# Linear attention and a gelu MLP on one core: batch 2's q mapped and transposed in two halves, and some steps of iteration 1 moved

## The chip, the cores and the metric

The kernel runs on one core of a Trainium2 chip. The metric is the device time of one execution in microseconds (us); the median of five runs is compared. TensorE is called PE in the profile, VectorE DVE, ScalarE ACT, GpSimd POOL and SyncE SP; SP's queue carries the loads and the DMA transposes here, ACT's queue the stores.

## The reference

Eight batches of eight heads, 576 positions, head width 64, go through linear attention; the result is the input of a two-layer MLP with 4608 rows, width 512 and inner width 2048:

```
phi(x) = where(x > 0, x, exp(x) - 1) + 1          # per element
kv  = phi(k)^T v ;  z = sum over positions of phi(k)
x   = (phi(q) kv) / (phi(q) z + 1e-6)             # per batch and head
h   = x @ w_in ;  g = gelu_tanh(h) ;  out = g @ w_out
```

## The kernel before, in words

phi(x) is made as min(max(x + 1, 1), exp(x)). So a map of q or k is three steps: `exp_of` on ACT, `linear_of` (add 1, maximum with 1) on DVE, `least_of` (the minimum of the two) on DVE. Tiles are [128 positions, chunks, heads, 64]: q has four chunks of 128 positions (the last 64 positions of each batch are handled later, two batches together), k has nine pieces.

For one batch the stages are: kv (`kv_paired`, 72 small matmuls into a pair of PSUM banks of its own, then casts into `kvbd` or `kv`); q transposed by DMA, chunk by chunk (`least_q`, from SP, into `qt`); n, the product of qt and kv (`nab`, one chunk at a time, L266), whose last column is the denominator; the division (`divide`, a reciprocal and a multiplication on DVE, L283 and L284) into `xs`; xs transposed by DMA into `xt` (`transposed_x`, L686); then the MLP on xt.

The MLP of one batch is an iteration of `iteration(j)`. It has 16 h tiles m0 to m15 (`h_mm`, L390, four matmuls of 128x512 each into one bank), each followed by a gelu on ACT (L405), and the output product. From iteration 1 on, the output product is made by seven half-size products of sums and differences (Winograd's form of Strassen's method): `sum_w_out` makes the sums of the weights once (L744), `Products.sums`, `third_sum` and `last_sum` those of g (L755, on DVE), and `Products.step(n)` one product of 16 matmuls (L782) and what follows it: a copy on ACT (L810, L823) or an addition on DVE (L851). Product 1's bank `p` is copied, and product 2 later accumulates into the same bank, so that bank is held from product 1 to the copy after product 2.

The order on every engine is written out by hand. `iteration(j)` makes a list of steps, and each step is a slot. Other work is put behind a slot with `at(j, slot, fn, ...)`, and `run(j, slot)` emits it, in the order in which it was registered; the plans of batches 2 and 3 are registered before those of the iteration itself. Iteration 1's slots are:

```
0-7: h m0-m7   8: product 1   9: product 7   10-17: h m8-m15   18-22: products 2, 6, 5, 4, 3
```

So h tile m11 is slot 13 and m13 is slot 15. In iteration 2 the h tiles alternate, m0, m8, m1, m9, and so on. While iteration 1 runs, the kernel prepares batch 2 (`plan_third`: its maps, kv at slot 12, n of chunks 0 to 3 at slots 15, 17, 18 and 18) and begins batch 3 and k of batch 4 (`plan_fourth`). An ACT table must be loaded when ACT changes between exp and gelu (L220 and L418).

h, the products and other one-bank tiles share six PSUM banks; a pair of banks of its own serves kv and most n tiles, one at a time. `load_*` calls put loads on SP's queue, seven buffers in turn; `least_q` also issues its four DMA transposes there (L663). The exp tile of k (`k_e`) has one buffer, so the exp of the next batch's k waits for the minimum that reads the one before.

Of the kernel before, what the change touches and what calls it, by code (L numbers as in the profile page):

```python
# [16 lines left out]
def kernel(  # L17
# [16 lines left out]
    nc = tc.nc  # L34
# [175 lines left out]
        n, hn = ld[name, b].shape[2] // D, ld[name, b].shape[1]  # L210
        phi[name, b] = pphi.tile([P, n, hn, D], BF16, name=name + "_p")

    def exp_of(name, b, hs=None):
        x = ld[name, b]
        hs = hs or slice(0, x.shape[1])
        if (name, b) not in exps:
            e = name + ("_e" if name != "qr" or b % 2 else "_f")
            exps[name, b] = pe.tile([P, x.shape[2] // D, x.shape[1], D], BF16, name=e)
        o, i = maps_view(name, b, x, exps[name, b], hs)
        nc.scalar.activation(o, i, AF.Exp)  # L220

    def linear_of(name, b, hs=None):
# [4 lines left out]
        o, i = maps_view(name, b, x, phi[name, b], hs)  # L227
        nc.vector.tensor_scalar(o, i, 1.0, 1.0, op0=ALU.add, op1=ALU.max)  # L228

    def least_of(name, b, hs=None):  # L230
        p, e = phi[name, b], exps[name, b]
        if hs:
            p, e = p[:, :, hs, :], e[:, :, hs, :]
        nc.vector.tensor_tensor(p, p, e, op=ALU.min)  # L234


# [276 lines left out]
    def at(j, slot, fn, *args):  # L513


        fill.setdefault((j, slot), []).append((fn, args))
# [74 lines left out]
    def plan_third():  # L591
        def n(c):
            transposed_x(2, c, (nab_in_banks if c == 3 else nab)(qts[2], 2, c))

        at(1, 1, sum_w_out, slice(0, 2))
        at(1, 2, linear_of, "k", 2)
        at(1, 3, linear_of, "q", 2)
        at(1, 4, cast_v, 2)
        at(1, 7, exp_of, "k", 2)
        at(1, 7, exp_of, "q", 2)  # L600
        at(1, 7, gelu_table)
        at(1, 9, least_of, "k", 2)
        at(1, 9, least_q, 2)
        at(1, 9, load_all_pairs, "k", k, 4)
        at(1, 12, kv_in_pair, 2)
        for c, slot in enumerate((15, 17, 18, 18)):
            at(1, slot, n, c)

    def plan_fourth():

        at(1, 12, linear_of, "k", 3)
        at(1, 17, exp_of, "k", 3)
        at(1, 18, exp_of, "q", 3)
        at(1, 18, exp_of, "k", 4)
        at(1, 18, gelu_table)
        at(1, 21, linear_of, "q", 3)
        at(1, 22, least_of, "k", 3)
        at(2, 0, cast_v, 3)
        at(2, 0, least_q, 3)
        at(2, 4, kv_in_pair, 3)  # L620
        at(2, 5, linear_of, "k", 4)
        at(2, 5, least_of, "k", 4)
        at(2, 5, cast_v, 4)
        at(2, 8, linear_of, "q", 4)
        at(2, 15, exp_of, "q", 4)
        at(2, 16, exp_of, "k", 5)
        at(2, 19, least_q, 4)
        at(2, 22, linear_of, "k", 5)
        at(3, 0, least_of, "k", 5)
# [26 lines left out]
        at(j, 15, exp_of, "qr", m)  # L656
        at(j, 18, least)

    def least_q(b):
        least_of("q", b)  # L660
        qts[b] = pt.tile([P, C, NP, P], BF16, name="qt")
        for c in range(C):
            nc.sync.dma_start_transpose(  # L663
                out=qts[b][:, c],
                in_=phi["q", b][:, c].rearrange("p h d -> p (h d)"),
            )
# [81 lines left out]
    class Products:  # L748
# [42 lines left out]
        def step(self, name):  # L791

            j = self.j
            (a11, a12), (a21, a22) = self.a
            (b11, b21), (t3, b22) = [[w_out_sb[:, d, h] for h in ff] for d in range(2)]
            t1, t2, t4 = (w_sum[:, i] for i in range(3))
            lo, hi = slice(0, N2), slice(N2, d_model)
            self.done = getattr(self, "done", ()) + (name,)

            def new():  # L800
                if name == 5 and j == B:
                    return [bank("o_ps", [P, N2]) for _ in range(2)]
                return bank("o_ps", [P, 2, N2])

            if name == 1:
                self.p = new()
                self.product(self.p, a11, b11, True)
                self.o1 = pout.tile([P, 2, d_model], FP32, name="o_sb")
                self.o2 = pout.tile([P, 2, d_model], FP32, name="o_sb")
                nc.scalar.copy(self.o1[:, :, hi], self.p)  # L810
            elif name == 5:
                self.z = new()
                self.product(self.z, self.s[0], t1, True)
            elif name == 6:
                v = new()
                self.product(v, self.s[1], t2, True)
                self.plus(self.o1[:, :, hi], v, self.o1[:, :, hi])
            elif name == 7:
                self.w = new()
                self.product(self.w, self.s3, t3, True)  # L820
            elif name == 2:
                self.product(self.p, a12, b21, False)
                nc.scalar.copy(self.o1[:, :, lo], self.p)  # L823
                if j == B:
                    self.store(0, self.o1, lo)
            elif name == 4:
                self.product(self.w, a22, t4, False)
                self.plus(self.o2[:, :, lo], self.w, self.o1[:, :, hi])
                self.store(1, self.o2, lo if j == B else slice(0, d_model))
            elif name == 3 and j < B:  # L830
                self.product(self.z, a11, b22, False)
                self.plus(self.o1[:, :, hi], self.z, self.o1[:, :, hi])
                at(j + 1, 0, self.store, 0, self.o1)
            elif name == 3:
                for t in range(2):
                    self.product(self.z, a11, b22, False, (t,))
                    self.plus(self.o1[:, t, hi], self.z[t], self.o1[:, t, hi])
                    self.store_rest(t, self.o1[:, t], hi)
            both = {6, 7} <= set(self.done)
            if name in (6, 7) and both:  # L840
                self.plus(self.o2[:, :, hi], self.w, self.o1[:, :, hi])
            if name in (5, 6, 7) and both and 5 in self.done:
                if j < B:
                    self.plus(self.o2[:, :, hi], self.z, self.o2[:, :, hi])
                else:
                    for t in range(2):
                        self.plus(self.o2[:, t, hi], self.z[t], self.o2[:, t, hi])
                    self.store(1, self.o2, hi)
# [20 lines left out]
    def iteration(j):  # L869
        xt = xts[j]  # L870
        if j < B:
            g = pg.tile([P, 2, MM, MAIN // 2], FP16, name="g")
        else:
            g = pg.tile([P, MM, 2, MAIN // 2], FP16, name="g").rearrange("p m a n -> p a m n")
        hs = [("h", m) for m in range(MM)]
        us = [range(m, m + 4) for m in range(0, MM, 4)]
        products = Products(j, g) if j else None
        early, late = slice(0, MM // 4), slice(MM // 4, MM // 2)
        if j == 0:
            us[2:3] = range(8, 10), range(10, 12)  # L880
            steps = hs + [("o", t, u) for u in us for t in range(C)]
        elif j == 1:
            steps = hs[:8] + [("product", n) for n in (1, 7)]
            steps += hs[8:] + [("product", n) for n in (2, 6, 5, 4, 3)]
            at(1, 7, products.third_sum, early, False)
            at(1, 7, products.third_sum, late, False)
            at(1, 7, sum_w_out, slice(2, 4))
            at(1, 13, products.sums, early)
            at(1, 17, products.sums, late)
            at(1, 19, products.last_sum)  # L890
        else:
            steps = [hs[i + n] for i in range(MM // 2) for n in (0, MM // 2)]
            steps += [("product", n) for n in (1, 5, 6, 7, 2, 4, 3)]
            for slot, ms in ((7, early), (15, late)):
                at(j, slot, products.sums, ms)
                at(j, slot, products.third_sum, ms)
            at(j, 16, products.last_sum)
        o_pss = {}
        for slot, step in enumerate(steps):
            if step[0] == "h":  # L900
                m = step[1]
                h_ps = h_begun.get(j, {}).get(m)
                if h_ps is None:
                    h_ps = bank("h_ps", [P, MAIN])
                    h_mm(h_ps, xt, m)
                gelu(j, g, m, h_ps)
            elif step[0] == "product":
                products.step(step[1])
            else:
                t, u = step[1:]  # L910
                if u.start == 0:
                    o_pss[t] = bank("o_ps", [P, d_model])
                o_mm(o_pss[t], g, t, u, half=(j, slot - 0.5))
                if u.stop == MM:
                    finish(j, t, o_pss[t])
            run(j, slot)
# [54 lines left out]
```

## Time and profile before

| | before |
|---|---|
| median of five runs | 272.74 us (272.39 to 272.83) |
| profiled execution | 272.4 us, of which span 270.6 us |
| PE busy | 264.2 us (98%) |
| PE weight load busy | 170.4 us (63%) |
| DVE busy | 164.9 us (61%) |
| ACT busy | 165.5 us (61%) |
| granted TensorE clock | 1.00 |
| iteration 1, first h to last product | 47.8 to 76.5 us |

Times in a timeline are counted from the start of the span. A row gives the start, the length, the engine, the line of the kernel, the operation and its tiles; equal neighbours are merged, with their number behind an x, and in brackets stands the idle time of the engine before the row with what ended it. Lengths of neighbouring instructions overlap: an h matmul is recorded with 0.38 us, but the next one starts 0.2155 us later. What an engine loses is therefore read from distances between starts.

### The profile page before, as it was taken

The numbers are of one execution on the slowest core, as the hardware profiler recorded it, in microseconds if no ns is written. First come the engines' busy times: TensorE is split into PE (matmuls) and PEld (weight loads), VectorE is DVE, ScalarE is ACT, GpSimd is POOL, SyncE is SP. The second block draws the span as 40 slices with busy tenths as digits, with TensorE's granted clock in tenths as the row PEclk, the third lists the DMA queues.
The fourth block names the chain that finished last, engine by engine and source line by source line (L and its number), as shares of the span: only waits on it lengthen the run. The fifth ranks groups of instructions, "written<-read, shape, count | busy, mean of one in ns | idle before, by whom it ended". The sixth has DMA issues, their size and how long they took to land.

```text
span 270.6 us, 5936 instructions
## 1 busy us (share of the span) xinstructions
PE 264.2 (98%) x2533; PEld 170.4 (63%) x2533; DVE 164.9 (61%) x263; ACT 165.5 (61%) x224; POOL 15.0 (6%) x21
## 2 busy tenths in 40 slices
PE   8999999999999999999999999999999999999994
PEld 3584456464854686558745874587458745874584
DVE  2860186988998966788738874683267316622262
ACT  4768877798839583669275926581665265028700
POOL 3056401000000000000000000000000000000000
PEclk9999999999999999999999999999999999999999
DMA  6999999993899998996698465217451312121004
GB/s 234 402 406 396 410 407 400 399 365 64 237 310 288 296 254 193 295 327 77 167 361 252 102 157 138 61 39 152 103 41 40 130 65 61 19 111 47 0 0 157
DMA packets 59786, 53.87 MB, mean 199 GB/s; under 512 B 35696, under 2 KB 45936, under 8 KB 59760
## 3 DMA queue, kind: packets, MB, share of 16 engines
q1 hardware_dynamic: 56880, 44.57, 57.1%
q10 hardware_dynamic: 2880, 8.91, 9.2%
q8 instruction: 20, 0.33, 0.5%
q14 instruction: 6, 0.05, 0.0%
HBM read 36.70 MB, written 9.44 MB: 170 GB/s over the span
## 4 chain that ended last, share of the span: by engine, by line
PE 90%; DMA 4%; ACT 1%; DVE 1%; SPq 1%; issue 0%; ACTq 0%
PE h_ps L390 44%; PE o_ps L782 36%; PE o_ps L726 5%; DMA v_x<-in_v_dram 3%; PE n_ps L328 1%; DMA qt<-q_p 1%; PE n_ps L250 1%; PE n_ps L266 1%; ACT k_e L220 1%; PE kv_ps L250 1%; PE t_ps L383 1%; SPq L94 1%; DVE k_p L234 1%; ACT L418 0%; SPq L99 0%
## 5 line engine op out<-in xcount | busy, mean ns | idle before, releaser
L390 PE MATMUL h_ps<-xt,w_in_sb 128*128 128x512 bf16 (+1 forms) x628 | 128.8, 361 | 0.6 <-ACT g L405 0.5
L405 ACT ACTIVATE g<-h_ps 128x512 f16<-128x512 f32 x144 | 86.2, 618 | 58.1 <-PE h_ps L390 56.2
L390 PEld LDWEIGHTS <-w_in_sb 128*128 128x128 bf16 x628 | 58.1, 98 | 63.1 <-issue 1.1
L782 PEld LDWEIGHTS <-g 128*128 128x128 f16 x624 | 60.9, 98 | 9.0 <-ACT g L405 0.2
L782 PE MATMUL o_ps<-w_out_sb,g 128*128 128x256 f16 x496 | 58.2, 273 | 0.0
L851 DVE TENSOR_TENSOR o_sb<-o_ps,o_sb 128x512 f32<-128x512 f32 (+1 forms) x42 | 27.9, 666 | 29.6 <-PE o_ps L782 28.7
L755 DVE TENSOR_TENSOR s<-g 128x1024 f16<-128x1024 f16 x18 | 12.5, 692 | 39.0 <-ACT g L405 39.0
L782 PE MATMUL o_ps<-w_sum,s 128*128 128x256 f16 x256 | 29.3, 273 | 0.0
L782 PEld LDWEIGHTS <-s 128*128 128x128 f16 x272 | 26.6, 98 | 3.0
L284 DVE TENSOR_TENSOR xs<-n_ps,r 128x384 bf16<-128x384 f32 (+2 forms) x44 | 25.6, 582 | 1.5
L220 ACT ACTIVATE k_e<-k_x 128x2304 bf16<-128x2304 f32 (+1 forms) x9 | 17.2, 1912 | 6.0 <-DVE k_p L234 5.2
L823 ACT COPY o_sb<-o_ps 128x512 f32<-128x512 f32 x8 | 4.7, 584 | 22.3 <-PE o_ps L782 22.3
L228 DVE TENSOR_SCALAR q_p<-q_x 128x2048 bf16<-128x2048 f32 (+1 forms) x9 | 9.9, 1102 | 13.4 <-DMA q_x<-in_q_dram 13.4
L220 ACT ACTIVATE q_e<-q_x 128x2048 bf16<-128x2048 f32 (+1 forms) x9 | 15.5, 1720 | 3.0 <-DMA q_x<-in_q_dram 3.0
L782 PE MATMUL o_ps<-w_sum,g 128*128 128x256 f16 x128 | 15.3, 272 | 0.0
L726 PE MATMUL o_ps<-w_out_sb,g 128*128 128x512 f16 x64 | 15.1, 379 | 0.0
L228 DVE TENSOR_SCALAR k_p<-k_x 128x2304 bf16<-128x2304 f32 (+1 forms) x9 | 11.0, 1220 | 4.2 <-DMA k_x<-in_k_dram 4.1
L418 ACT ACT_TABLE_LOAD x9 | 11.5, 1283 | 0.2
L234 DVE TENSOR_TENSOR k_p<-k_p,k_e 128x2304 bf16<-128x2304 bf16 (+1 forms) x9 | 11.0, 1221 | 0.8 <-ACT k_e L220 0.4
L755 DVE TENSOR_TENSOR s<-s,g 128x1024 f16<-128x1024 f16 x16 | 11.1, 692 | 0.5
L239 DVE CAST vp<-v_x 128x2304 bf16<-128x2304 f32 (+1 forms) x9 | 11.0, 1225 | 0.5 <-DMA v_x<-in_v_dram 0.4
L427 PE MATMUL w_ps<-warm 128*128 128x512 bf16 x32 | 10.0, 469 | 1.2 <-DVE warm L182 1.2
(62 smaller groups left out, 150.7 us busy)
## 6 DMA issues: line engine op xcount, KB each, us to landing
out_dram<-o_sb ACTq DMA_DIRECT2D x16, 512.0 KB, 4.8
k_x<-in_k_dram SPq DMA_DIRECT2D x7, 1152.0 KB, 7.3
v_x<-in_v_dram SPq DMA_DIRECT2D x7, 1152.0 KB, 12.2
q_x<-in_q_dram SPq DMA_DIRECT2D x6, 1024.0 KB, 11.7
w_st<-in_moe_w_in_dram SPq DMA_DIRECT2D x3, 1024.0 KB, 13.2
q_x<-in_q_dram SPq DMA_DIRECT2D x4, 512.0 KB, 8.8
w_st<-in_moe_w_out_dram SPq DMA_DIRECT2D x2, 1024.0 KB, 12.5
w_st<-in_moe_w_out_dram SPq DMA_DIRECT2D x4, 512.0 KB, 11.3
```

The costliest lines, as they stand in the source:

```text
L220: nc.scalar.activation(o, i, AF.Exp)
L228: nc.vector.tensor_scalar(o, i, 1.0, 1.0, op0=ALU.add, op1=ALU.max)
L234: nc.vector.tensor_tensor(p, p, e, op=ALU.min)
L239: fn(out=vp_paired(b)[:, :, us, 0:D].rearrange("p j u d -> p u j d"), in_=ld["v", b][:, us].rearrange("p u (j d) -> p u j d", d=D),)
L284: nc.vector.tensor_tensor(x_v, n_v[heads + (slice(0, D),)], r[heads + (None,)].to_broadcast(shape + [D]), op=ALU.mult,)
L390: nc.tensor.matmul(h_ps[:, ts], lhsT=w_in_sb[:, c, P * m : P * (m + 1)], rhs=xt[:, c, ts], start=(c == 0), stop=(c == KM - 1), skip_group_ ...
L405: nc.scalar.activation(g_v, h_v, AF.Gelu_apprx_tanh)
L418: nc.scalar.preload_act_table_set("gelu_apprx_tanh_and_others")
L726: nc.tensor.matmul(o_ps, lhsT=g[:, t // 2, m, P * (t % 2) : P * (t % 2 + 1)], rhs=w_out_sb[:, :, m, :], start=(m == 0), stop=(m == MM - 1),)
L755: nc.vector.tensor_tensor(out, i0, i1, op=op)
L782: nc.tensor.matmul(ps[t] if type(ps) is list else ps[:, t, :], lhsT=lhs[:, m, P * t : P * (t + 1)], rhs=rhs[:, m, :], start=(first and m = ...
L851: nc.vector.tensor_tensor(out, i0, i1, op=ALU.add)
```

## The change

In iteration 1, batch 2's q is mapped in two halves of two chunks each: the exp of chunks 0 and 1 comes before the exp of k, that of chunks 2 and 3 behind it; the minimum of the first half is taken at slot 8, with two DMA transposes behind it, that of the second half at slot 9 with the other two. The last of the four weight sums moves from slot 7 to slot 8. kv of batch 2 moves from slot 12 to 13 (behind h m11). The linear part of batch 3's k is taken in two halves of head pairs, at slots 9 and 13, instead of whole at slot 12, and its minimum at slot 20 instead of 22. The ACT copy of product 1 moves from slot 8 to slot 13, and the first sums of g from slot 13 to 14.

```diff
-    def exp_of(name, b, hs=None):
+    def exp_of(name, b, hs=None, cs=None):
...
         o, i = maps_view(name, b, x, exps[name, b], hs)
+        if cs:
+            o, i = o[..., cs, :], i[..., cs, :]
         nc.scalar.activation(o, i, AF.Exp)
...
-    def least_of(name, b, hs=None):
+    def least_of(name, b, hs=None, cs=None):
...
+        if cs:
+            p, e = p[:, cs], e[:, cs]
         nc.vector.tensor_tensor(p, p, e, op=ALU.min)
...
         at(1, 4, cast_v, 2)
+        at(1, 7, exp_of, "q", 2, None, slice(0, 2))
         at(1, 7, exp_of, "k", 2)
-        at(1, 7, exp_of, "q", 2)
+        at(1, 7, exp_of, "q", 2, None, slice(2, C))
         at(1, 7, gelu_table)
+        at(1, 8, least_q, 2, slice(0, 2))
         at(1, 9, least_of, "k", 2)
-        at(1, 9, least_q, 2)
+        at(1, 9, least_q, 2, slice(2, C))
         at(1, 9, load_all_pairs, "k", k, 4)
-        at(1, 12, kv_in_pair, 2)
+        at(1, 13, kv_in_pair, 2)
...
-        at(1, 12, linear_of, "k", 3)
+        for slot, hs in zip((9, 13), halves):
+            at(1, slot, linear_of, "k", 3, hs)
...
+        at(1, 20, least_of, "k", 3)
         at(1, 21, linear_of, "q", 3)
-        at(1, 22, least_of, "k", 3)
...
-    def least_q(b):
-        least_of("q", b)
-        qts[b] = pt.tile([P, C, NP, P], BF16, name="qt")
-        for c in range(C):
+    def least_q(b, cs=slice(0, C)):
+        least_of("q", b, cs=cs)
+        if b not in qts:
+            qts[b] = pt.tile([P, C, NP, P], BF16, name="qt")
+        for c in range(cs.start, cs.stop):
...
-                nc.scalar.copy(self.o1[:, :, hi], self.p)
+                if j == 1:
+                    at(1, 13, nc.scalar.copy, self.o1[:, :, hi], self.p)
+                else:
+                    nc.scalar.copy(self.o1[:, :, hi], self.p)
...
-            at(1, 7, sum_w_out, slice(2, 4))
-            at(1, 13, products.sums, early)
+            at(1, 7, sum_w_out, slice(2, 3))
+            at(1, 8, sum_w_out, slice(3, 4))
+            at(1, 14, products.sums, early)
```

## The prediction, made before the changed kernel was run

> **What bounds the kernel now.** I read the page first. Its engine line and the heaviest group say that TensorE (PE) is busy nearly always, with h and output products:
>
> ```profile
> PE 264.2 (98%) x2533; PEld 170.4 (63%) x2533; DVE 164.9 (61%) x263; ACT 165.5 (61%) x224; POOL 15.0 (6%) x21
> ```
>
> So an edit can give time only where PE waits. The chain of waits in order of time shows two such places after the first batches, both in or just behind iteration 1 (columns: start, length, what):
>
> ```profile
> 60.90 0.71 PE kv_ps L250 x72
> 61.60 0.30 PE h_ps L390
> 61.91 3.06 DMA qt<-q_p
> ...
> 65.02 0.41 PE n_ps L266 x4
> ...
> 77.32 1.36 DVE k_p L234
> 78.68 0.02 issue
> 78.70 2.13 ACT k_e L220
> ```
>
> From 105.22 on the same chain holds nothing but PE until the last store. How much PE loses I take from its timeline around these places, by start-to-start distances (an h matmul takes 0.2155, twelve between 58.14 and 60.83):
>
> ```profile
> 60.83 0.78 PE L250 MATMUL kv_ps<-vp,k_p 64*64 64x65 bf16 x72
> 61.54 1.04 PE L390 MATMUL h_ps<-xt,w_in_sb 128*128 128x512 bf16 x4
> 63.03 1.89 PE L390 MATMUL h_ps<-xt,w_in_sb 128*128 128x512 bf16 x8 [0.46 <-ACT g L405]
> 65.02 0.41 PE L266 MATMUL n_ps<-kvbd,qt 128*128 128x130 bf16 x4
> ```
>
> h11 starts at 61.54, so h12 could at 62.41; it starts at 63.03: **0.62** lost, waiting for gelu 8 to free a bank. h12 and h13 end their issue at 64.76, the first n starts at 65.02: **0.26** lost, for the first transposed chunk of qt, which lands at 64.97. In iteration 2 h10 starts at 81.64 and h3 could at 82.51; the chain has it at 82.79: **0.28** lost, behind gelu 0 (82.14 to 82.75), exp k4 (78.70) and least k3 (77.32). Sum 1.16 us: the ceiling of any gain here. The timelines of ACT, DVE and SP show what stands in front:
>
> ```profile
> 56.66 2.13 ACT L220 ACTIVATE k_e<-k_x 128x2304 bf16<-128x2304 f32 x1
> 58.69 1.90 ACT L220 ACTIVATE q_e<-q_x 128x2048 bf16<-128x2048 f32 x1
> 60.60 1.28 ACT L418 ACT_TABLE_LOAD   x1
> 61.90 0.59 ACT L810 COPY o_sb<-o_ps 128x512 f32<-128x512 f32 x1
> 62.38 3.17 ACT L405 ACTIVATE g<-h_ps 128x512 f16<-128x512 f32 x6
> ```
>
> ```profile
> 60.62 1.23 DVE L234 TENSOR_TENSOR q_p<-q_p,q_e 128x2048 bf16<-128x2048 bf16 x1 [0.44 <-ACT q_e L220]
> ...
> 64.48 0.69 DVE L755 TENSOR_TENSOR s<-g 128x1024 f16<-128x1024 f16 x1 [0.47 <-ACT g L405]
> ```
>
> ```profile
> 61.91 5.89 SPq L663 DMA_TRANSPOSE qt<-q_p  x4
> 67.91 0.52 SPq L94 DMA_DIRECT2D k_x<-in_k_dram  x1
> ```
>
> The copy sits ahead of gelu 8; the four transposes wait for the whole q minimum; the sums of slot 13 wait for gelu 11.
>
> **Part by part.** *ACT, slot 7.* The order becomes exp q2 (two chunks), exp k2, exp q2 (the other two), table, gelu 8. Halves of 1024 occur in the first batch: 1.058 us each against 1.909 whole; with the 0.10 by which neighbouring ACT instructions overlap, the split costs 0.96 + 0.96 - 1.81, about 0.1. Starts: q2a 56.66, k2 57.61, q2b 59.64 (ends 60.70), table 60.72, gelu 8 at 62.01 without the copy in front (before 62.38), its end 62.61, so the bank is free for h12 at 62.66. The nearest rows could make the split cost nothing (60.60 for the table) or 0.2 (two whole lengths): h12 between 62.55 and 62.75.
>
> [...]
>
> *The copy of product 1 (0.59, 0.48 start to start)* goes behind gelu 11 (slot 13). It is hidden there: it ends near 64.5, gelu 13 and 14 then wait for their matmuls anyway (ACT idles 0.77 before 66.32). Its reader, product 2's accumulation, starts after 66.5. If that cover were gone it would cost 0.48.
>
> *DVE, slots 7 to 9.* sum_w_out is only divided between slots: no cost. q2a's minimum (0.69, first batch) runs at 57.75, in the idle time before least k2; then the last weight sum until 59.59. least k2 waits for exp k2, now 0.95 later: 59.77 to 61.13. The rest of q2's minimum 61.04 to 61.73, first half of linear k3 (0.75) to 62.40; k3 landed at 58.91.
>
> *PE, kv.* It moves from behind h10 to behind h11. h11 starts at 60.73 (h10 at 59.87), kv at 61.69, 0.56 after its keys are ready, and ends issue at 62.40: it fills most of the hole that stood there. h12 starts at 62.66, **0.37** earlier. Evacuation of kv (two casts, 0.86) 62.50 to 63.36, second half of linear k3 until 64.14.
>
> *SP.* Two transposes can be issued at 58.4 instead of 61.91. All loads ahead of them have been issued, but v3 is still moving (landed 61.58). The pair issued in traffic at 81.14 landed at 87.16, 1.67 behind the q4 load (85.49); the one at 61.91 needed 3.06. So chunk 0 lands between 61.5 (58.4 + 3.06) and 64.4 (58.4 + 6.0, the longest of all qt rows); I take 63.0, v3's end plus 1.5. n0 wants it at 62.66 + 1.72 + 0.03 = 64.41 and kvbd at 63.4: no wait is left, and n0 is **0.60** earlier. The second pair issues at 61.75 and lands by about 66.2; n2 uses it after 68. The k4 load behind them then issues near 64.3 instead of 67.91, and xt's transposes queue behind a load that is finished sooner: no cost, no gain, since xt lands at 75.93 against a need at 76.5.
>
> *What is late next: n1.* It uses the bank pair of n0 and so waits for n0's division on DVE, and that stands behind the two sums of slot 13, now slot 14, which need gelu 11 (start 63.46, end 64.07; before 64.44). Sums start at 64.11 against 64.48; from there to the end of the division the rows take 2.39 (64.48 to 66.87): 66.50, n1 at 66.55. PE could at 66.42. Before it was 67.02. So only **0.47** of the 0.60 survives iteration 1 (0.3 if DVE's extra halves come 0.15 later, 0.60 if it keeps up).
>
> *End of iteration 1.* least k3 moves ahead of two output additions. Before, exp k4 idled 5.20 for it; now it runs after the addition of product 5 (74.02 before, 73.55 now), at 74.2 to 75.5. exp k4 then ends at 77.7, the table at 79.0, gelu 0 at 79.6, against h3's need at 82.0: the **0.28** goes, with 2.4 to spare. The additions of products 4 and 3 come 0.5 later relative to PE; product 4's bank is free at 76.1 and product 3's at 77.9. Banks are handed out again in the order in which they were freed, so these two go to the fifth and sixth h of iteration 2, which start at 79.5 and 81.2: 3.4 and 3.3 of margin. The store that waits for product 4's addition is issued from ACT's queue at about 76.2, ahead of gelu 0, and holds nothing up. DVE's work up to the divisions of iteration 2 keeps its sum.
>
> Sum: 0.47 + 0.28 = 0.75. The profiled execution took 272.4 (span 270.6), the median of the runs 272.74, 0.34 more; I carry the difference over: 272.74 - 0.75 = **272.0**.
>
> **Rivals.** *Little arrives.* PE is at 98%, and 0.47 of the gain passes through three engines' handshakes. If n0 or n1 waits as late as before (qt chunk 0 near 65, or DVE's sums not sooner), only the 0.28 stays: 272.46, by my bound no change. For it: DVE has no idle 0.15 left between 61.0 and 66.5. Against: every step has a row.
>
> *Slower: the second half's minimum waits for the first half's transposes.* Both touch the same tile q_p. If that write waits for chunk 1 to be read, landing about 63.2, it starts 2.2 late on DVE's queue; linear k3, the kv evacuation, the sums and the division stand behind it. kv's evacuation starts at 64.45, ends at 65.3, the rest of linear k3 at 65.95, sums at 66.0 instead of 64.48, n1 1.5 later than before, less 0.28: 273.9. It decides from a landing of chunk 1 after about 62.0. Against: the divisions of iteration 2 write further chunks of xs until 93.0 while a transpose of its chunk 0, issued at 91.00, lands only at 101.62, and DVE does not wait.
>
> **How the numbers follow.** About 0.2% (0.55 us) is what this measurement can tell from no change. Forecast 0.66 (0.62 of it faster by more than that, 0.04 within); little arrives 0.22; slower 0.12, nearly all by that mechanism or by a qt that lands after 65.9. Faster 0.62, same 0.26, slower 0.12. Low end: all 1.16 recovered, 271.6, and 0.1 of spread. High end: the second case plus its spread, 272.7. That leaves out the slower case and some tail.
>
> **What would show it.** PE: kv after h11, h12 near 62.7, n0 near 64.4, n1 near 66.55 with DVE's division as its releaser, no hole before iteration 2's seventh h. ACT: no 5.2 of idle before exp k4. SP: two transposes at 58.4. I am wrong if n0 still waits for qt, if DVE idles between the two q2 minima until a transpose lands, or if a new wait appears after 90.

## The result, and the profile after

The changed kernel takes 271.90 us in the median of 19 runs (271.65 to 272.25), the kernel before, over the same comparison, 272.69 us (37 runs, 272.26 to 273.24). The ratio is 0.9973 with a 95% interval of 0.9967 to 0.9979: 0.79 us between the medians, 0.57 to 0.90 us by the interval. The forecast was 272.0. The lowest times differ by 0.61 us, the highest by 0.99.

The page of the changed kernel reports 0.8 us less PE time and a span of 270.4 us; its profiled execution took 272.24 us, which is one of its slower ones, while that of the kernel before (272.4) is one of its faster ones.

```profile
PE 263.4 (97%) x2533; PEld 170.3 (63%) x2533; DVE 165.2 (61%) x265; ACT 166.0 (61%) x225; POOL 14.5 (5%) x21
```

In the chain of waits in order of time, around the place of the change, the DMA of qt is gone, and so is the run of DVE, ACT and table ahead of gelu 0. What stands there instead is DVE, between kv and n1 (h is L394 now, kv L254, n L270):

```profile
62.01 0.91 PE kv_ps L254 x72
...
62.94 0.42 DVE kvbd L686
...
63.85 0.76 DVE k_p L230
64.61 0.61 DVE s L763
...
65.24 0.69 DVE s L763
...
66.21 0.70 DVE xs L288
66.91 0.14 issue
67.04 0.40 PE n_ps L270 x4
...
81.73 7.01 PE h_ps L394 x32
```

The last line is the repaired hole of iteration 2: 32 h matmuls in 7.01, where the row before needed 7.36 (81.64) with a pause inside. PE's timeline gives the distances:

```profile
58.39 3.62 PE L394 MATMUL h_ps<-xt,w_in_sb 128*128 128x512 bf16 x16
61.94 0.78 PE L254 MATMUL kv_ps<-vp,k_p 64*64 64x65 bf16 x72
62.89 1.89 PE L394 MATMUL h_ps<-xt,w_in_sb 128*128 128x512 bf16 x8 [0.17 <-issue]
64.61 0.40 PE L270 MATMUL n_ps<-kvbd,qt 128*128 128x130 bf16 x4
64.85 1.89 PE L394 MATMUL h_ps<-xt,w_in_sb 128*128 128x512 bf16 x8
67.04 0.40 PE L270 MATMUL n_ps<-kvbd,qt 128*128 128x130 bf16 x4 [0.31 <-DVE xs L288]
```

The whole trace after lies 0.25 us later here than the one before, though no step of PE ahead of this place was changed (h8 starts at 58.39, before at 58.14; over all profiles of this study between 57.79 and 58.39). So I count from h8's first matmul from now on. h12 starts 4.50 after it (before 4.89), n0 6.22 (6.88), n1 8.65 (8.88), and the span ends 211.98 after it (212.48). h12's remaining wait is 0.24, n0 has none, and n1 has a new one of 0.44, released by the division on DVE. On SP the transposes begin at 58.76 instead of 61.91, as the view of SP's queue shows; its row merges all four, of which the second pair begins at 62.00:

```profile
58.76 5.75 SPq L671 DMA_TRANSPOSE qt<-q_p  x4
64.61 0.52 SPq L94 DMA_DIRECT2D k_x<-in_k_dram  x1
```

So the profiled stretch became 0.50 shorter, the median 0.79. The experiments look for what n1's wait is, what each part gives, and where the difference between 0.50 and 0.79 comes from. The table lists all profiles, in us from h8; "c0, c1" is the time from issue to landing of the first two transposes of qt (a dash: no landing in the trace); the spread is highest less lowest of the timed runs.

| kernel | n0 | n1 | end | c0, c1 | median (before beside it) | spread |
|---|---|---|---|---|---|---|
| before | 6.88 | 8.88 | 212.48 | 3.06, 2.38 | 272.69 | 0.98 |
| before_again | 6.97 | 8.94 | 212.55 | 3.16, 2.39 | one run, 272.26 | |
| only_copy | 7.05 | 9.02 | 212.62 | 3.24, 2.39 | 272.31 (272.50) | 0.89 |
| only_least | 6.62 | 9.02 | 212.35 | 2.39, 3.86 | 272.19 (272.27) | 1.49 |
| whole_q | 6.20 | 9.82 | 213.53 | 2.38, 4.66 | 272.85 (272.27) | 1.17 |
| halves_only | 6.71 | 8.96 | 212.58 | 3.89, 3.02 | 272.27 (272.50) | 0.22 |
| copy_back | 6.70 | 8.96 | 212.28 | 3.66, - | 272.04 (272.27) | 0.37 |
| least_back | 6.21 | 8.65 | 212.24 | 3.92, 3.03 | 272.01 (272.56) | 0.22 |
| after | 6.22 | 8.65 | 211.98 | 3.51, - | 271.90 (272.69) | 0.60 |
| after_again | 6.22 | 8.64 | 211.96 | 3.87, 2.98 | 271.76 (272.56) | 0.46 |
| k3b_20 | 6.22 | 8.47 | 211.79 | 3.71, - | 271.53 (272.56) | 0.21 |
| kv_12 | 6.34 | 8.47 | 211.79 | 3.89, 2.97 | 271.64 (272.50) | 0.26 |
| sums_15 | 6.22 | 8.18 | 211.71 | 3.90, 2.98 | 271.38 (272.27) | 0.20 |
| sums15_k3b20 | 6.22 | 8.18 | 211.70 | 3.90, 3.01 | 271.52 (272.56) | 0.36 |

### The profile page after: what moved, and what is told of

Its sections match the earlier page's. It is cut to its first block, busy times and chain, and to the rows that moved or that the text cites. A ratio compares the mean times of both kernels' runs of the same rounds, so it can differ in the third digit from the quotient of the medians.

```text
span 270.4 us, 5941 instructions
## 1 busy us (share of the span) xinstructions
PE 263.4 (97%) x2533; PEld 170.3 (63%) x2533; DVE 165.2 (61%) x265; ACT 166.0 (61%) x225; POOL 14.5 (5%) x21
## 4 chain that ended last, share of the span: by engine, by line
PE 92%; DMA 3%; DVE 2%; SPq 1%; issue 0%; ACT 0%
PE h_ps L394 45%; PE o_ps L790 36%; PE o_ps L734 5%; DMA v_x<-in_v_dram 3%; PE n_ps L332 1%; PE kv_ps L254 1%; PE n_ps L254 1%; PE n_ps L270 1%; PE t_ps L387 1%; SPq L94 1%; DVE s L763 0%; SPq L99 0%; PE t_ps L545 0%; DVE kvbd L686 0%; DVE vp L243 0%
## 5 line engine op out<-in xcount | busy, mean ns | idle before, releaser
L394 PE MATMUL h_ps<-xt,w_in_sb 128*128 128x512 bf16 (+1 forms) x628 | 128.4, 361 | 0.2 <-issue 0.2
L394 PEld LDWEIGHTS <-w_in_sb 128*128 128x128 bf16 x628 | 58.1, 98 | 62.5
L238 DVE TENSOR_TENSOR q_p<-q_p,q_e 128x2048 bf16<-128x2048 bf16 (+1 forms) x10 | 10.1, 1007 | 1.0 <-ACT q_e L222 0.9
```

The source lines that it names most:

```text
L394: nc.tensor.matmul(h_ps[:, ts], lhsT=w_in_sb[:, c, P * m : P * (m + 1)], rhs=xt[:, c, ts], start=(c == 0), stop=(c == KM - 1), skip_group_ ...
```

## Experiments: each part by itself

**least k3 alone (only_least), and the change without it (least_back).**

```diff
-        at(1, 22, least_of, "k", 3)
+        at(1, 20, least_of, "k", 3)
```

> The kernel before with one part of the change alone: least k3 at slot 20 instead of 22. Theory (the gain is the sum of three PE waits, and this part owns the one before iteration 2's seventh h): exp k4, its table and gelu 0 come 2.6 us sooner, h3 starts without a wait, 0.28 us faster than before, 272.4 where before is 272.7. Rival (all of the gain arises in iteration 1, and this hole only moves to the next bank): 272.7, and the profile shows a new wait of about 0.3 us among the h tiles of iteration 2.

> The changed kernel with least k3 back at slot 22. Theory (this part alone fills the hole before h3 of iteration 2): a hole of 0.2 to 0.3 us comes back there, 0.2 to 0.3 slower than the changed kernel of this call. Rival (run alone on the kernel before it gave 0.08 with an interval that holds zero, so it gives nothing): no difference.

Alone, the time didn't settle it: the ratio is 0.9995, the interval 0.9984 to 1.0007. Taken out of the changed kernel it is clearer: least_back has a ratio of 0.9977 (0.9967 to 0.9987) where the changed kernel beside it has 0.9971 (0.9961 to 0.9982), and medians of 272.01 against 271.76; the intervals overlap, but six of the changed kernel's seven times lie below all eleven of least_back. The traces agree with each other to 0.01: from n1 to the end it takes 203.60 in the kernel before and 203.33 in only_least, 203.59 in least_back and 203.33 in the changed kernel. The idle of ACT for this minimum is back in least_back, in the view of ACT around 80:

```profile
78.35 2.12 ACT L222 ACTIVATE k_e<-k_x 128x2304 bf16<-128x2304 f32 x1 [5.64 <-DVE k_p L238]
```

In the changed kernel exp k4 idled 2.94. This term is 0.27 to 0.28, where 0.28 was predicted. In only_least it was hidden by a wait of n1 that I had not foreseen:

```profile
64.50 0.40 PE L266 MATMUL n_ps<-kvbd,qt 128*128 128x130 bf16 x4
64.73 1.89 PE L390 MATMUL h_ps<-xt,w_in_sb 128*128 128x512 bf16 x8
66.90 0.41 PE L266 MATMUL n_ps<-kvbd,qt 128*128 128x130 bf16 x4 [0.28 <-DMA qt<-q_p]
```

Here chunk 0 came in time and chunk 1 late. Up to n1 this program has the order of the kernel before, so that wait can occur in the kernel before too. No profile of the kernel before has it, though. A second one (before_again) was taken for this; n1 was expected between 8.87 and 9.8 after h8, with the landing of a chunk as what ends the wait, or, as the rival, at 8.87 again. It came at 8.94, close to the rival's number and without a wait of n1, and again it was chunk 0 that was late, by about the same:

```profile
64.89 0.41 PE L266 MATMUL n_ps<-kvbd,qt 128*128 128x130 bf16 x4 [0.19 <-DMA qt<-q_p]
65.14 1.89 PE L390 MATMUL h_ps<-xt,w_in_sb 128*128 128x512 bf16 x8
66.86 0.40 PE L266 MATMUL n_ps<-kvbd,qt 128*128 128x130 bf16 x4
```

**q whole again (whole_q).**

```diff
-        at(1, 7, exp_of, "q", 2, None, slice(0, 2))
         at(1, 7, exp_of, "k", 2)
-        at(1, 7, exp_of, "q", 2, None, slice(2, C))
+        at(1, 7, exp_of, "q", 2)
...
-        at(1, 8, least_q, 2, slice(0, 2))
         at(1, 9, least_of, "k", 2)
-        at(1, 9, least_q, 2, slice(2, C))
+        at(1, 9, least_q, 2)
```

> The changed kernel with batch 2's q exponentiated, minimised and transposed in one piece again (after k, minimum and four transposes at slot 9), all other parts kept. Theory: the first transpose issues near 62 and lands near 65.2, n0 starts there instead of at 64.6, n1 can't start before 67.3 instead of 67.04: 0.25 us slower than the changed kernel, 272.15. Rival (the half transposes are the whole gain in iteration 1): 0.5 slower, 272.4. Second rival (DVE sets n1 anyway): 271.9.

All three theories missed: the ratio is 1.0017 (1.0006 to 1.0028), slower than the kernel before. n0 found its chunk in time; n1 waited. PE's timeline:

```profile
64.12 0.41 PE L270 MATMUL n_ps<-kvbd,qt 128*128 128x130 bf16 x4
64.36 1.89 PE L394 MATMUL h_ps<-xt,w_in_sb 128*128 128x512 bf16 x8
67.74 0.41 PE L270 MATMUL n_ps<-kvbd,qt 128*128 128x130 bf16 x4 [1.49 <-DMA qt<-q_p]
...
69.73 0.45 PE L270 MATMUL n_ps<-kvbd,qt 128*128 128x130 bf16 x5
```

By distances n1 is 1.62 late. Chunk 1 was issued at 63.03 and landed at 67.69, 4.66 later. DMA was all but idle for much of that time, and in the same window one packet of another queue stands among the transposes'; the DMA view of 63.03 to 67.69:

```profile
DMA  9998110000199999990000000000000100038999
...
q1 hardware_dynamic: 1547, 0.38, 67.9%
q8 instruction: 1, 0.02, 2.3%
```

The trace's packet records place that packet (16,384 bytes, on queue 8, whose kind the view gives as instruction, so a fetch of instructions) at 64.36, and it lasts 1.70. Every one of the five profiles with q whole has one such packet near a transpose that is late: at 62.05 to 62.37 in before, before_again and only_copy, where chunk 0 takes 3.06 to 3.24 instead of 2.38 to 2.39; at 64.36 and 64.76 in whole_q and only_least, where chunk 1 takes 4.66 and 3.86. So either n0 or n1 waits, and the amount differs between the profiles. The kernels with the halves fit: in the three of them that have such a packet at 63.17 to 63.53 (copy_back, k3b_20, sums_15) chunk 2 takes 3.83 to 4.37, in the six that have it at 69.09 or later chunk 2 takes 2.29 to 2.30. There the late chunk costs nothing, since it lands by 7.98 after h8 and n2 starts at 10.16 at the earliest. That the fetch causes the delay is read from this coincidence; no run moves the fetch alone, and why it delays a chunk by more than its own length I did not test.

It is also open whether the fetch moves from one execution of a kernel to the next. The two kernels that were profiled twice have it at the same place both times: 4.23 and 4.17 after h8 in the kernel before, 11.21 and 11.30 in the changed one. In only_least, which has the order of the kernel before up to n1, it comes at 6.88.

The lateness in whole_q also goes on: SP issues the four transposes until 68.4, the loads of batch 4 follow later, qt of batch 3 lands from 88.59 to 90.08, and the n matmuls of iteration 2 take 1.04 there instead of 0.66.

**The halves alone (halves_only).** The kernel before with only these lines of the change:

```diff
+        at(1, 7, exp_of, "q", 2, None, slice(0, 2))
         at(1, 7, exp_of, "k", 2)
-        at(1, 7, exp_of, "q", 2)
+        at(1, 7, exp_of, "q", 2, None, slice(2, C))
...
+        at(1, 8, least_q, 2, slice(0, 2))
         at(1, 9, least_of, "k", 2)
-        at(1, 9, least_q, 2)
+        at(1, 9, least_q, 2, slice(2, C))
...
-            at(1, 7, sum_w_out, slice(2, 4))
+            at(1, 7, sum_w_out, slice(2, 3))
+            at(1, 8, sum_w_out, slice(3, 4))
```

> The kernel before with only q of batch 2 in halves (exp, minimum, transposes, and the last weight sum at slot 8 behind the first minimum); kv at slot 12, linear k3 whole, the copy at slot 8, least k3 at 22, the sums at 13 as before. Theory (the halves take away the dependence on qt's landing, but no other wait): n0 without a wait for qt, kv 0.3 us late because its keys come later, h12 0.1 later, n1 at 8.9 to 9.0 us from h8 since the sums wait for gelu 11; the lowest times like the lowest of before, but the spread under 0.5 us where before has 1.2, so the median 0.1 to 0.4 faster than before. Rival (the halves themselves shorten the path): 0.5 or more faster. Second rival (only a cost without the other moves): slower than before.

The profiled stretch is no shorter (212.58 against 212.48 and 212.55), kv waits 0.35 for its keys, h12 0.37 for its bank, and n1 comes at 8.96. Yet the median is 0.23 lower than that of before beside it (ratio 0.9991, 0.9982 to 1.0000), and the eleven runs spread over 0.22 where the 21 of before spread over 0.83. All of this is as expected, but the interval just reaches 1. By these runs, what the halves alone take away is spread, and no part of the profiled stretch.

**The copy alone (only_copy), and the change without it (copy_back).** The second diff, against the changed kernel:

```diff
-                if j == 1:
-                    at(1, 13, nc.scalar.copy, self.o1[:, :, hi], self.p)
-                else:
-                    nc.scalar.copy(self.o1[:, :, hi], self.p)
+                nc.scalar.copy(self.o1[:, :, hi], self.p)
```

> The kernel before with only the copy of product 1 moved to slot 13. Theory (h12 gains 0.45 us, but n0 and n1 then stand for qt, which is not sooner): no difference to before in the median, the same spread of over 1 us; n1 not earlier than 8.8 us from h8. Rival (the copy is the larger part of the gain): 0.4 faster.

> The changed kernel with the copy of product 1 back at slot 8. Theory (n1 is what is late, and it stands behind the sums that need gelu 11): every gelu from 8 on is 0.48 us later, h12 and n0 0.48 later, the sums 0.26 later because DVE was not ready sooner, n1 0.26 later: 0.26 us slower than the changed kernel, about 272.15. Rival (DVE alone sets n1, so the copy hides nothing): the time of the changed kernel, 271.9. Second rival (h12's bank sets the pace): 0.48 slower, 272.4.

In only_copy the ratio is 0.9992 (0.9983 to 1.0001), no difference, as expected; the spread, 0.89, is a little under the 1 us expected. h12 starts 4.40 after h8 instead of 4.89, and n0 gives all of it back to qt:

```profile
61.33 2.89 PE L390 MATMUL h_ps<-xt,w_in_sb 128*128 128x512 bf16 x12
64.99 0.41 PE L266 MATMUL n_ps<-kvbd,qt 128*128 128x130 bf16 x4 [0.76 <-DMA qt<-q_p]
```

In copy_back the ratio is 0.9985 (0.9975 to 0.9994), and n1 comes at 8.96 instead of 8.65, so 0.31 in the trace against 0.26 expected. The sums now wait for gelu 11, as DVE's timeline says:

```profile
64.48 0.69 DVE L763 TENSOR_TENSOR s<-g 128x1024 f16<-128x1024 f16 x1 [0.22 <-ACT g L409]
```

By the traces the copy is worth 0.3 with the halves and nothing without them.

## Experiments: what holds n1 in the changed kernel

**A second look (after_again).** The changed kernel, unaltered.

> The changed kernel once more, beside the three that follow, and for a second profile of it. Theory after the first four runs (in the kernel before, n0 or n1 waits for a qt chunk whose landing differs from one execution to the next, 2.4 to 4.7 us after its issue; in the changed kernel chunks 0 and 1 are issued 3.5 us sooner and only DVE holds n1): 0.5 to 0.9 us faster than before, and n1 again released by the division, about 0.4 us late. Rival (n1's lateness in the changed kernel was an accident of one execution): n1 starts without a wait.

The ratio is 0.9971 (0.9961 to 0.9982). The distances repeat within 0.01, n1's wait is 0.43 and again released by the division. It is no accident.

**The sums behind n0's division (sums_15), linear k3's second half later (k3b_20), and both.**

```diff
-            at(1, 14, products.sums, early)
+            at(1, 15, products.sums, early)
```

```diff
-        for slot, hs in zip((9, 13), halves):
+        for slot, hs in zip((9, 20), halves):
```

> The changed kernel with the first sums of g behind n0's division on DVE (slot 15) instead of ahead of it (slot 14). Theory (the hole of 0.43 us before n1 is the division waiting behind the sums): n0's division ends near 66.0, n1 starts without a wait, 0.3 to 0.43 us faster than the changed kernel, 271.5 to 271.6, a little of it given back to product 6, whose second sums come 0.2 us later on DVE. Rival (DVE is full from 61 to 74, so that what n1 gains n2 or product 6 loses): 271.9.

> The changed kernel with the second half of linear k3 at slot 20, right ahead of its minimum, instead of slot 13. Theory (that half, 0.76 us, stands between the kv evacuation and the sums on DVE, and gelu 11 would allow the sums 0.2 us sooner): n1 0.15 to 0.2 us sooner, 0.15 to 0.2 faster than the changed kernel of this call; the minimum, exp k4 and gelu 0 come 0.65 later, which their 2.4 us of margin take. Rival (n1 is bound by gelu 11 alone): no difference.

> The changed kernel with both: the first sums behind n0's division (slot 15) and the second half of linear k3 at slot 20. Theory: n1 has no wait left, only 0.24 us before h12 remains; 0.4 to 0.5 us faster than the changed kernel of this call. Moving linear k3 adds nothing to moving the sums, since DVE is idle 0.44 us ahead of n0's division in that version. Rival (the two add up): 0.6 faster.

sums_15 has the lowest ratio of all, 0.9961 (0.9947 to 0.9975); the intervals of all four kernels of this section reach into that of the changed kernel, so the sizes below are those of the traces. n1 starts without a wait at 8.18, 0.47 sooner, and the end comes 0.27 sooner than in the changed kernel, a little under the 0.3 to 0.43 expected. DVE now idles ahead of n0's division instead of having it wait:

```profile
64.50 0.21 DVE L287 RECIPROCAL r<-n_ps 128x8 f32<-128x8 f32 x1 [0.44 <-PE n_ps L270]
64.75 0.69 DVE L288 TENSOR_TENSOR xs<-n_ps,r 128x512 bf16<-128x512 f32 x1
65.35 0.68 DVE L763 TENSOR_TENSOR s<-g 128x1024 f16<-128x1024 f16 x1
```

Of the 0.47, then, 0.20 is not there at the end. It goes in the products behind n3: the 32 matmuls of products 6 and 5 and the step to product 4 take 3.76 instead of 3.56. 0.07 of it is a pause inside product 6, whose second sums DVE now ends later, and 0.12 one ahead of product 4, which waits for the second addition that reads its bank (DVE 70.78 to 72.19, product 4 at 72.24). In k3b_20 the ratio is 0.9965 (0.9953 to 0.9978), and n1 and the end both come 0.18 sooner, as expected. With both the ratio is 0.9963 (0.9951 to 0.9976) and the end at 211.70 as with the sums alone; they don't add up, as expected, but the gain on the changed kernel, 0.24 in the medians, is under the 0.4 to 0.5 expected. Against the kernel before, sums_15 is 0.89 us faster beside it (271.38 against 272.27).

**kv back at slot 12 (kv_12).**

```diff
-        at(1, 13, kv_in_pair, 2)
+        at(1, 12, kv_in_pair, 2)
```

> The changed kernel with kv of batch 2 back at slot 12. Theory: PE waits 0.3 us for least k2 there, and h12, which waited for its bank, loses only 0.1; DVE evacuates kv 0.5 us sooner, the sums are then bound by gelu 11, and n1 comes 0.1 to 0.2 us sooner: the same time as the changed kernel or 0.15 faster. Rival (the move of kv is what fills the hole before h12, and without it n1 is late): 0.3 slower than the changed kernel.

The ratio is 0.9965 (0.9953 to 0.9978) and the end 0.18 sooner than in the changed kernel. PE pauses for the keys, but DVE evacuates kv at 62.05, 4.16 after h8 instead of 4.55, and n1 gains 0.17:

```profile
60.92 0.78 PE L254 MATMUL kv_ps<-vp,k_p 64*64 64x65 bf16 x72 [0.28 <-DVE k_p L238]
61.63 2.76 PE L394 MATMUL h_ps<-xt,w_in_sb 128*128 128x512 bf16 x12
```

So in the company of the other parts the move of kv costs 0.18 in the trace: it fills PE's hole and makes DVE, which is late, later.

## Why the prediction was right, and where only its total was

The terms, in us from h8, and what the traces of before and after show, from unrounded times:

| step | predicted | measured |
|---|---|---|
| h12 sooner | 0.37 | 0.39 |
| n0 sooner | 0.60 | 0.65 |
| n1 sooner, what survives | 0.47 | 0.22 |
| hole before h3 of iteration 2 | 0.28 | 0.28 |
| sum | 0.75 | 0.50 |
| between the medians | 0.75 | 0.79 (0.57 to 0.90) |

*ACT.* The split costs 0.11 from start to start (0.96 and 1.06 for the halves, 1.91 for the whole), near the 0.1 taken from the first batch. The recorded lengths add up to more (1.06 and 1.04 against 1.90, so 0.20), but that is not what the split costs in time: neighbours overlap, the first half and the exp of k by 0.10 (56.91 + 1.06 against 57.87). The copy held nothing up: ACT still idles 0.27 for its matmul before gelu 15.

*n1, the term that was mis-sized.* The step named the right engine and the right queue (division behind the sums), and the size was 0.25 too large. Two hand-overs were too short in it. I let kv's evacuation start 0.03 after kv's recorded end (61.69 + 0.78 to 62.50); it started 0.22 after it (62.72 to 62.94). No row of the kernel before shows 0.22: in iteration 1 DVE was busy when kv ended, and in iteration 2, where DVE was idle, the cast came 0.07 after the recorded end (81.70 to 81.77). With an idle DVE the profiles have 0.06 to 0.23 for this pair of steps; what decides it stays open. And n1 followed the division by 0.14 (66.91 to 67.04) where I had 0.05. k3b_20 and sums_15 show that the chain is the one that was named.

*qt.* Chunk 0 landed at 62.27, earlier than the 63.0 taken; n0 did not wait. What I missed lies in the kernel before: I read the landings of chunks 0 and 1 from one execution and took them for constants. The five profiles with q whole show 2.38 to 3.24 for chunk 0 and 2.38 to 4.66 for chunk 1, and a wait of n0 or n1 behind the late one. In the kernels with the halves, chunks 0 and 1 land no later than 4.74 after h8 in every profile that records it, and are needed at 6.2 and 8.2 at the earliest. That the missing 0.29 between 0.50 and 0.79 is this wait is supported by the lowest times, which differ by 0.61 only, by the spreads (0.83 to 1.49 with q whole, in 11 to 37 runs; 0.20 to 0.60 with halves, in 5 to 19) and by halves_only, whose median gains 0.23 with no gain in its profiled stretch; how often the late case happens was not counted. That it is this wait, and this wait alone, is not shown: in the nine rows of the table with halves the gain between the medians exceeds that of the profiled stretch by 0.03 (copy_back) to 0.34 (k3b_20), and in the three changed rows with q whole the excess runs from -0.05 (only_least) to 0.47 (whole_q). By the profiles the opening doesn't explain it, since h8 starts at 57.96 in the mean of the five profiles with q whole and at 58.00 in the mean of the nine with halves. That the total came out right was luck: one term was 0.25 too large, and something of about that size was left out.

*The slower rival* didn't occur: in after_again the second half's minimum starts at 60.68, straight behind least k2, while chunk 1 of the first half lands at 62.47. *The rival of little gain* was half true: n1 kept less than I had said.

*End of iteration 1.* exp k4 started at 76.03 and gelu 0 ended 2.46 before h3 needed its bank (2.4 predicted). The later additions held nothing up: in iteration 2 the first 20 h matmuls take 4.48 from 76.54 and the next 32 7.08 from 81.66, without a pause. *SP's queue* was costed at nothing, which the changed kernel bears out; but whole_q shows a price of lateness there, 0.38 at the n matmuls of iteration 2.

## What to carry to other kernels

Where a matmul waits for a small transfer, look at that transfer's landing in several executions: one profile shows which chunk was late that time, not how late it can be (here chunk 1 took 2.38 to 4.66 with q whole), and a wide spread of the timed runs is a sign worth following (here 0.83 to 1.49 with q whole, 0.20 to 0.60 with halves). When an edit moves work off the engine that waits, follow the next engine's own queue in order: here filling PE's hole with kv delayed DVE, which was the one that was late, and taking the sums behind the division on DVE (sums_15) gave 0.27 where undoing that move gave 0.18. Where a gain hangs on a hand-over between two engines, carry its delay as a range: here the same pair of steps had 0.06 to 0.23.

## What the runs showed of the hardware

The transpose of one chunk (128x512 in bf16, 131,072 bytes) landed 2.36 and 2.38 us after its issue in the kernel before (chunks 2 and 1) and 2.29 in the changed one (chunk 2), where no load and no fetch moved beside it. The chunk that was late took 3.06 to 4.66 in the eight profiles in which a 16,384-byte instruction fetch of 0.97 to 1.70 us falls near it, and chunk 0 took 3.51 to 3.92 in the nine with halves, where it is issued while the load of v3 still moves (that load lands at 61.46 to 61.70). In whole_q the delay is 2.28 over the 2.38 of an undisturbed landing, longer than the fetch's 1.70; by what means a fetch could hold up a transpose, no run here shows.

The opening of the kernel, in which PE's steps are the same in all versions, ends between 57.79 and 58.39 us by the start of h8. That alone is nearly as large as the effect studied, and the reason for counting from h8.
